# LSH attention and two MoE layers on one core: weight tiles rebuilt with a parametric ReLU, and tiles, transposes and the last x moved

## Chip, cores and metric

One core of a Trainium2 chip. The metric is the device time of one execution in microseconds (us), the median over several executions.

## What is computed

`q`, `k`, `v` are 2 x 8 heads x 768 positions x 64, float32; the weights are float64.

```python
q_bits = (einsum('bhsd,dk->bhsk', q, proj) > 0); k_bits likewise     # 6 bits, a bucket
mask = q_bucket[:, :, :, None] == k_bucket[:, :, None, :]
scores = where(mask, scale * q @ k.T, -1e9)
x = softmax(scores) @ v                 # laid out as 1536 tokens x 512
h = x @ w_in;  x = (h * sigmoid(1.702 * h)) @ w_out          # layer 1, d_ff 2048
h = x @ w_in2; out = (h * tanh(log1p(exp(h)))) @ w_out2      # layer 2
```

## The kernel before, in words

Every float32 operand of a product is split into a rounded high part and a low part, and a product is three matmuls (high x high, high x low, low x high).

**Attention.** `NSTEP` = 96 steps: 16 heads of 6 steps (`NT`), each step a block of 128 queries. In step i, `clamp` (L369) takes the scores out of PSUM on VectorE, `expo` (L380) exponentiates on ScalarE, and three steps later `trp` (L417, L424) transposes the probabilities on TensorE and copies out their high part on ScalarE, `trl` (L429) makes their low part on VectorE, and `pv` (L441, L442) multiplies by v. `ORDER` sets the order of the pieces in a step; its letter `T` runs what the table `todo` has for that step. `at(step, f, ...)` fills that table. `prep(n)` readies head n: `s0`, `s1` and `s3` are GpSimd work (L251 to L258, L328), `s2` is the bucket logits on TensorE (L266) and their compare into `mk` on VectorE (L280), `s4` and `s5` are DMAs of the results into `qb` and `kb`. Head 0 has a path of its own, `first` (L295 to L320), that runs before step 0, with head 1's k copied by `mid` (L335) in its middle. `x_out` and `x_split` normalise two finished heads on GpSimd and split them into `x_hi` and `x_lo`; for the last pair they run inside the MoE loop, at i of 4 and 6. After step 95 four more steps, called the drain here, finish transposes and products; each also holds a quarter of the first two `gemm_in`.

**Weight tiles.** 64 tiles of 128 x 512 float64 make up both layers (`wlist`; tile number k). `wload` loads one, and the generator `wsplit` turns it into float32 high and low parts in six stages; `wgo(k, n)` runs the next n:

```python
nc.scalar.mul(wf, hw.bitcast(F32), REBIAS)                                          # L112 ScalarE
nc.vector.tensor_scalar(lw, lw, 29, None, ALU.logical_shift_right)                  # L114 VectorE
nc.vector.scalar_tensor_tensor(lw, wb, 3, lw, ALU.logical_shift_left, ALU.bitwise_or)       # L116
nc.vector.scalar_tensor_tensor(wb, wb, 0x80000000, lw, ALU.bitwise_and, ALU.bitwise_or)     # L118
nc.scalar.copy(hi, wf)                                                              # L126 ScalarE
sub(lo, wf, rnd(hi))                                                                # L128
```

Before, `NPRE` = 5 tiles are made during attention, one per two heads: they run in heads 5 to 6, 7 to 8, 9 to 10, 11 to 12 and 13 to 14 (heads counted from 0), with the low part on GpSimd. The `at` calls of L528 to L532 set their steps.

**MoE.** Loop i runs `gemm_in(i)` (12 matmuls of 512 columns, L159), `act(i - 1)` (two ACTIVATEs on ScalarE, L600 and L601, and a subtraction on VectorE, L602) and `gemm_out(i - 2)` (12 matmuls, L618). There are 96 i: 2 layers x 3 chunks of 512 tokens x 16 blocks of d_ff. In the first chunk of layer 1, `conv(i)` gives two tiles to each loop, and the loop interleaves their stages with `act`. `gp` holds the activated blocks, three of each part.

Of the kernel before, what the change touches and what calls it, by code (L numbers as in the profile page):

```python
# [10 lines left out]
F32 = mybir.dt.float32  # L11
# [9 lines left out]
SET_GELU = 12  # L21
SET_MISH = 25
REBIAS = float(2.0**-112)


def mask_consts():
# [10 lines left out]
def lsh_attention_moe_kernel(  # L37
# [13 lines left out]
    P = 128  # L51
# [6 lines left out]
    NCH = NTOK // CH  # L58
    NW0 = 1
    XO = 11  # L60
    NPRE = 5
    NW1 = KF - 3
    QSCALE = -1.0 / float(D) ** 0.5

# [14 lines left out]
    def rnd(ap):  # L79
        return ap.bitcast(F32)  # L80
# [25 lines left out]
    def wsplit(k, sub):  # L106
        m, f, j = wlist[k]
        raw = raw_t.pop(k)
        lw, hw = raw[:, :, 0], raw[:, :, 1]
        wf = wr.tile([P, DM], F32, tag="wb", name="wb")  # L110
        wb = wf.bitcast(U32)
        nc.scalar.mul(wf, hw.bitcast(F32), REBIAS)  # L112
        yield
        nc.vector.tensor_scalar(lw, lw, 29, None, ALU.logical_shift_right)  # L114
        yield
        nc.vector.scalar_tensor_tensor(lw, wb, 3, lw, ALU.logical_shift_left, ALU.bitwise_or)  # L116
        yield
        nc.vector.scalar_tensor_tensor(wb, wb, 0x80000000, lw, ALU.bitwise_and, ALU.bitwise_or)  # L118
        yield
        n0 = NW0 + 3 * (j == 0)  # L120
        pi = 0 if f < n0 else 1 if f < NW1 else 2
        nb = (n0, NW1 - n0, KF - NW1)[pi]
        hi = wpools[pi].tile([P, DM], F32R, tag=f"wh{j}", name="wh", bufs=nb)
        lo = wpools[pi].tile([P, DM], F32R, tag=f"wl{j}", name="wl", bufs=nb)
        w_t[m, f, j] = (hi, lo)
        nc.scalar.copy(hi, wf)  # L126
        yield
        sub(lo, wf, rnd(hi))  # L128

    def wfetch(upto):  # L130
        while wstate["load"] < min(upto, len(wlist)):
            wload(wstate["load"])
            wstate["load"] += 1
# [30 lines left out]
    def attention():  # L164
        with ExitStack() as es:
# [16 lines left out]
            def load_q(n):  # L182
                b, h = divmod(n, H)
                t = nat.tile([P, S], F32, tag="qn", name="qn")
                nc.sync.dma_start(t[0:D], qt[b, h])
                nat_t["q", n] = t

            def load_k(n):
                b, h = divmod(n, H)
                t = nat.tile([P, S], F32, tag="kn", name="kn")  # L190
                nc.sync.dma_start(t, kt[b, h])
                nat_t["k", n] = t

            def load_v(u):
# [3 lines left out]
                nat_t["v", u] = t  # L198

            load_table(SET_EXP_LN)  # L200
            load_q(0)
            pjt = pp.tile([P, 3, 64], F32, tag="p", name="pjt")
            nc.sync.dma_start(pjt, pj)
            load_k(0)
            mc = cst.tile([P, 2], F32, name="mc")
            nc.sync.dma_start(mc, mconst)
# [3 lines left out]

            ident = cst.tile([P, P], F32, name="ident")
            make_identity(nc, ident)
            zero = pp.tile([P, 2, HS], F32, tag="p", name="zero").rearrange("p a b -> p (a b)")
            nc.vector.memset(zero[32:64], 0.0)
            qb_tiles = [cst.tile([P, S], F32R, name=f"qb{i}") for i in range(2)]
# [21 lines left out]
            def prep(n):  # L237
# [57 lines left out]
                def first(mid):  # L295
                    prep_w()
                    nc.vector.tensor_scalar(qk_m[0:D], qn[0:D], QSCALE, None, ALU.mult)
                    nc.scalar.mul(qx[D:P], qn[0:D], QSCALE)
                    nc.vector.scalar_tensor_tensor(
                        qx[0:D], qn[0:D], QSCALE, rnd(qk_m[0:D]), ALU.mult, ALU.subtract  # L300
                    )
                    pts = []
                    for f in range(2):
                        c = slice(f * HS, (f + 1) * HS)
                        nc.scalar.copy(kh[:, c], kn[:, c])
                        nc.vector.tensor_sub(qk_m[D:P, c], kn[D:P, c], rnd(kh[D:P, c]))
                    nc.scalar.copy(qb[D:P], rnd(qx[D:P]))
                    pcopy(kb[D:P], rnd(qk_m[D:P]))
                    for f in range(2):
                        c = slice(f * HS, (f + 1) * HS)  # L310
                        pts.append(ps_t.tile([P, 512], F32, tag="pt", name="pt"))
                        logits(pts[f], f, 64, True, True)
                    mid()
                    for f in range(2):
                        c = slice(f * HS, (f + 1) * HS)
                        nc.vector.tensor_scalar(
                            qb[0:64, c], pts[f][0:64, :HS], mc[0:64, 0:1], mc[0:64, 1:2],
                            ALU.is_gt, ALU.mult,
                        )
                        nc.scalar.copy(kb[0:32, c], rnd(qb[32:64, c]))  # L320
# [140 lines left out]
            def x_out(u):  # L461
                ul = xs_t[u]
                uh = uh_t.pop(2 * u)
                rb = rb_t.pop(u)
                nc.gpsimd.tensor_add(ul, ul, uh)
                nc.gpsimd.tensor_mul(ul, ul, rb)

            def x_split(u):
                ul = xs_t.pop(u)
                b, hp = divmod(u, NPAIR)  # L470
                t0, t1 = b * S, (b + 1) * S
                while t0 < t1:
                    c, o = divmod(t0, CH)
                    n = min(CH - o, t1 - t0)
                    xh = x_hi[c][:, hp, o : o + n]
                    src = ul[:, t0 - b * S : t0 - b * S + n]
                    pcopy(xh, src)
                    nc.gpsimd.tensor_sub(x_lo[c][:, hp, o : o + n], src, rnd(xh))
                    t0 += n

            first, first_v = prep(0)
            second = prep(1)
            first(second[1])
# [8 lines left out]
            def at(step, f, *args):  # L492
                todo.setdefault(step, []).append((f, args))
# [3 lines left out]

            at(1, first_v)

            for f, st in zip(second[3:], (1, 7, 1, 2)):  # L500
                at(st, f)

            def start_prep(n):
# [21 lines left out]
                at(NT * (n + 1) + NZ, norm2, n)  # L525
                at(NT * (n + 1) + NZ + 2, norm3, n)

            for k in range(NPRE):  # L528
                st = NSTEP - 4 - 2 * NT * (NPRE - k)
                at(st - 10, wfetch, k + 1)  # L530
                for off in (-1, 0, 2, 5, 8, 9):
                    at(st + off, wgo, k, 1, nc.gpsimd.tensor_sub)  # L532
            for j in range(3):
                at(st - 4 + 6 * j, wfetch, NPRE + 1 + j)
            at(NSTEP, load_table, SET_GELU)

            qk(0)
# [39 lines left out]
            for st in sorted(todo):  # L577
                for f, args in todo[st]:
                    f(*args)
            late.append(lambda: x_out(NHD // 2 - 1))  # L580
            late.append(lambda: x_split(NHD // 2 - 1))

    def moe():
        with ExitStack() as es:
            gp = es.enter_context(tc.tile_pool(name="gp", bufs=3))
            wpools[1] = es.enter_context(tc.tile_pool(name="w1", bufs=NW1))
            ps_y = es.enter_context(tc.tile_pool(name="ps_y", bufs=1, space=PSUM))
            N = len(steps)
# [55 lines left out]
            def conv(i):  # L644
                if i < KF:
                    return list(range(2 * i + 1, min(2 * i + 3, 2 * KF)))
                if i < LAST + 3:
                    return []
                a, b = (3 * (i - LAST - 3 + d) // 2 for d in (0, 1))
                return list(range(2 * KF + min(a, 2 * KF), 2 * KF + min(b, 2 * KF)))  # L650

            act(0)
            wgo(conv(2)[0], 1)
            for i in range(2, N + OLAG):
                if i == NH + 1:
                    load_table(SET_MISH)
                if i < KF and i in (4, 6):
                    late.pop(0)()
                if i == 9:
                    es_u.close()  # L660
                    wpools[2] = es.enter_context(tc.tile_pool(name="w2", bufs=KF - NW1))
                if i < N:
                    gemm_in(i)
                k1, k2 = (conv(i) + [None, None])[:2]
                if k1 is not None:
                    wgo(k1, 2)
                    for k in conv(i - 1)[1:]:
                        wgo(k, 1)
                    wgo(k1, 1)
                    wfetch(k1 + 4)  # L670
                elif i > 2:
                    for k in conv(i - 1)[1:]:
                        wgo(k, 1)
                if i - 1 < N:
                    act(i - 1)
                if k2 is not None:
                    wgo(k2, 1)
                if k1 is not None:
                    wgo(k1, 1)
                if k2 is not None:  # L680
                    wgo(k2, 2)
                if k1 is not None:
                    wgo(k1, 1)
                if k2 is not None:
                    wgo(k2, 1)
                    wfetch(k2 + 4)
                for k in conv(i + 1)[:1]:
                    wgo(k, 1)
                if k2 is not None:
                    wgo(k2, 1)  # L690
                gemm_out(i - OLAG)

    attention()
# [58 lines left out]
```

## Time and profile before

| what | value |
|---|---|
| median of 3 runs | 773.44 us (773.33 to 774.28) |
| the profiled execution's own time | 774.58 us |
| its span, first to last instruction | 772.7 us |
| TensorE, matmuls | 748.9 us busy (97%), 3760 instructions |
| VectorE | 431.8 us busy (56%), 791 instructions |
| ScalarE | 382.1 us busy (49%), 780 instructions |
| GpSimd | 186.4 us busy (24%), 189 instructions |
| chain that ended last | TensorE 79%, GpSimd 6%, VectorE 5%, issue 4%, DMA 3%, ScalarE 2% |

Matmuls are pipelined, so TensorE's busy time counts a matmul's whole flight and some of the gaps between two. The granted TensorE clock is printed as 1.0 over the whole span.

### The profile page before, as it was taken

To read this page: it belongs to the slowest core of one execution; us is meant where nothing else is said; L and a number is where in the kernel's file an instruction comes from. 1 tells how busy PE (TensorE), PEld (TensorE's weight loads), DVE (VectorE), ACT (ScalarE), POOL (GpSimd) and SP (SyncE) were. 2 spreads that over 40 slices of the span, in tenths; PEclk is the share of its full clock that TensorE was granted. 3 is DMA by queue.
4 is the path that set the end of the run, shared out by engine and by line. 5 is a ranking of instruction groups with operands and counts; after the bars stand their busy time and mean duration, and the time that the engine had idled before them with its cause. 6 is when DMAs were issued, how large, how long until landed. Compare 5 with 4: busy or idle time off the path is not lost.

```text
span 772.7 us, 10578 instructions
## 1 busy us (share of the span) xinstructions
PE 748.9 (97%) x3760; PEld 645.5 (84%) x3760; DVE 431.8 (56%) x791; ACT 382.1 (49%) x780; POOL 186.4 (24%) x189
## 2 busy tenths in 40 slices
PE   5999998999999899999999999999999999999998
PEld 4999998898898688888888888888888888888886
DVE  6988999899995999921111877779111211111111
ACT  5888888787786466632212554556211221222121
POOL 7767887788732400000000000000000000000000
PEclk9999999999999999999999999999999999999999
DMA  6576567475431466600000344534000100010001
GB/s 166 144 188 171 153 163 165 131 189 149 140 100 42 128 204 196 198 22 1 0 1 1 109 137 137 163 99 148 0 1 1 54 1 1 0 55 1 0 1 55
DMA packets 25892, 69.77 MB, mean 90 GB/s; under 512 B 4432, under 2 KB 6576, under 8 KB 25840
## 3 DMA queue, kind: packets, MB, share of 16 engines
q1 hardware_dynamic: 25840, 69.11, 31.2%
q8 instruction: 29, 0.48, 0.3%
q14 instruction: 23, 0.19, 0.1%
HBM read 49.38 MB, written 3.19 MB: 68 GB/s over the span
## 4 chain that ended last, share of the span: by engine, by line
PE 79%; POOL 6%; DVE 5%; issue 4%; DMA 3%; ACT 2%; SPq 1%; DVEq 0%; POOLq 0%; ACTq 0%
PE y L618 33%; PE h L159 33%; PE s L356 4%; PE pt L417 4%; PE u L442 2%; PE u L441 2%; DMA qn<-in_qt_dram 2%; DVE p L369 1%; PE prep L266 1%; ACT p L380 1%; DVE raw L116 1%; DVE ptl L429 1%; POOL qk_m L251 1%; POOL qk_m L258 1%; POOL qx L254 1%
## 5 line engine op out<-in xcount | busy, mean ns | idle before, releaser
L602 DVE TENSOR_TENSOR gl<-h,gh 128x512 fp32r<-128x512 f32 x96 | 66.2, 690 | 270.7 <-ACT h L601 270.2
L600 ACT ACTIVATE gh<-h 128x512 fp32r<-128x512 f32 x96 | 57.3, 597 | 255.6 <-PE h L159 255.6
L159 PE MATMUL h<-x_hi,wl 128*128 128x512 f32 x384 | 149.6, 389 | 0.9 <-DVE wl L128 0.9
L159 PE MATMUL h<-x_hi,wh 128*128 128x512 f32 x384 | 149.5, 389 | 0.0
L159 PE MATMUL h<-x_lo,wh 128*128 128x512 f32 x384 | 149.4, 389 | 0.0
L429 DVE TENSOR_TENSOR ptl<-pt,pth 128x384 fp32r<-128x384 f32 x192 | 98.0, 552 | 23.7 <-ACT pth L424 23.6
L380 ACT ACTIVATE p<-p,mn 128x768 f32<-128x768 f32 x96 | 91.1, 949 | 14.7 <-DVE p L369 14.3
L424 ACT CAST pth<-pt 128x384 fp32r<-128x384 f32 x192 | 83.0, 485 | 28.9 <-PE pt L417 28.5
L369 DVE TENSOR_SCALAR_CACHE_REDUCE p<-s 128x768 f32<-128x768 f32 x96 | 90.4, 943 | 2.2 <-PE s L356 2.2
L417 PE MATMUL pt<-ident,p 128*128 128x128 f32 x576 | 82.6, 274 | 8.9 <-DVE ptl L429 6.4
L159 PEld LDWEIGHTS h<-x_hi,wl 128*128 128x128 f32 x384 | 72.0, 187 | 16.3 <-DVE wl L128 1.3
L159 PEld LDWEIGHTS h<-x_hi,wh 128*128 128x128 f32 x384 | 72.1, 188 | 15.0 <-issue 0.2
L159 PEld LDWEIGHTS h<-x_lo,wh 128*128 128x128 f32 x384 | 72.1, 188 | 14.8
L417 PEld LDWEIGHTS pt<-ident,p 128*128 128x128 f32 x576 | 67.8, 140 | 18.4 <-DVE ptl L429 9.3
L618 PE MATMUL y<-gh,wl 128*128 128x512 f32 x192 | 75.0, 390 | 1.1 <-DVE wl L128 1.1
L618 PE MATMUL y<-gl,wh 128*128 128x512 f32 x192 | 74.8, 389 | 0.0
L618 PE MATMUL y<-gh,wh 128*128 128x512 f32 x192 | 74.7, 389 | 0.0
L618 PE MATMUL y<-wh,gh 128*128 128x512 f32 x192 | 74.7, 389 | 0.0
L618 PE MATMUL y<-wl,gh 128*128 128x512 f32 x192 | 74.7, 389 | 0.0
L618 PE MATMUL y<-wh,gl 128*128 128x512 f32 x192 | 74.7, 389 | 0.0
L441 PE MATMUL u<-pth,vv 128*128 128x384 f32 x192 | 64.9, 338 | 0.0
L442 PE MATMUL u<-ptl,vv 128*128 128x384 f32 x192 | 64.7, 337 | 0.0
(84 smaller groups left out, 1118.0 us busy)
## 6 DMA issues: line engine op xcount, KB each, us to landing
raw<-in_wt_dram SPq DMA_DIRECT2D x64, 512.0 KB, 3.6
kn<-in_kt_dram SPq DMA_DIRECT2D x16, 384.0 KB, 5.2
qn<-in_qt_dram SPq DMA_DIRECT2D x16, 192.0 KB, 6.5
vn<-in_vt_dram SPq DMA_DIRECT2D x8, 384.0 KB, 5.3
ul<-uh SPq DMA_DIRECT2D x16, 192.0 KB, 3.9
rb<-scr SPq DMA_DIRECT2D x16, 192.0 KB, 3.5
out_dram<-ob SPq DMA_DIRECT2D x12, 256.0 KB, 2.1
qx<-qk_m SPq DMA_DIRECT2D x15, 192.0 KB, 4.8
```

Source lines behind the costliest of these rows:

```text
L159: nc.tensor.matmul(h, a[:, wk], x[:, kk], start=(n == 0), stop=(n == 3 * KD - 1))
L356: nc.tensor.matmul(s[:, f, :HS], a[:, c], bb[:, f * HS : (f + 1) * HS], start=st, stop=not st,)
L369: nc.vector.tensor_scalar(sb, s[:, :, :HS], NEG, None, ALU.min, ALU.min, accum_out=mn)
L380: nc.scalar.activation(p, p, AF.Exp, bias=mn, scale=-1.0, accum_out=z_t[n][:, t : t + 1],)
L417: nc.tensor.transpose(ptile[:, j * P : (j + 1) * P], p_t[3 * g + j][:, t * P : (t + 1) * P], ident,)
L424: nc.scalar.copy(hi, ptile[:, :HS])
L429: nc.vector.tensor_sub(lo, ptile[:, :HS], rnd(hi))
L441: nc.tensor.matmul(ut[:, :HS], vv[:, t, :], hi, start=(t == 0), stop=False)
L442: nc.tensor.matmul(ut[:, :HS], vv[:, t, :], lo, start=False, stop=(t == NT - 1))
L600: nc.scalar.activation(gh, h, fn)
L602: nc.vector.tensor_sub(gl, h, rnd(gh))
L618: nc.tensor.matmul(y[j], w[:, js] if m == 0 else x[:, js], x if m == 0 else w, start=(first and n == 0), stop=(last and n == 2),)
```

## The change

- **Weight tiles.** For all tiles but the last five, stage 1 becomes a parametric ReLU on ScalarE whose slope for negative inputs is 2^32. Together with the later shift by 3 it puts the sign in place, so the second OR on VectorE (L118 before) is gone: five stages instead of six.
- **Where tiles are made.** Two tiles are still made during attention (heads 11 to 12 and 13 to 14). Tiles 2, 3 and 4 are made in step 95 and the drain, low part on VectorE (`DRAIN`).
- **The last x.** The last pair's `x_out` goes to VectorE at i = 7 (`x_last`), its split to ScalarE and VectorE in two pieces at i = 14 and 20 (`x_tail`). The buffer `xl` for it is new, and `gp` goes from three buffers to two.
- **The start.** 24 transposes of the identity into a scratch tile run on TensorE before its first use. `pjt` is loaded first; head 0's k is loaded as two halves of 64 partitions (before: 128 partitions at once), and its upper copy is made on ScalarE. Head 1's logits and mask go from steps 1 and 2 to steps 2 and 3.
- **Layer 2's tiles** are made two to a loop (before: three to two loops).

```diff
+NEGBIT = float(2.0**32)
-    NPRE = 5
+    NPRELU = 4 * KF - 5
+    DRAIN = (
+        (-1, 2, 1), (0, 2, 2), (0, 3, 1), (1, 2, 1), (1, 3, 2), (1, 4, 1), (2, 2, 1), (2, 3, 1),
+        (2, 4, 2), (3, 3, 1), (3, 4, 1), (4, 4, 1),
+    )
+    NWARM = 24
...
-        nc.scalar.mul(wf, hw.bitcast(F32), REBIAS)
+        if k < NPRELU:
+            nc.scalar.activation(wf, hw.bitcast(F32), AF.Prelu, scale=REBIAS, alpha=NEGBIT)
+        else:
+            nc.scalar.mul(wf, hw.bitcast(F32), REBIAS)
...
+        if k < NPRELU:
+            nc.vector.scalar_tensor_tensor(wb, wb, 3, lw, ALU.logical_shift_left, ALU.bitwise_or)
+        else:
...
+                if n == 0:
+                    for f in range(2):
+                        c = slice(f * HS, (f + 1) * HS)
+                        nc.sync.dma_start(t[0:D, c], kt[b, h, 0:D, c])
...
+            warm = ps_t.tile([P, 512], F32, tag="pt", name="warm")
+            for _ in range(NWARM):
+                nc.tensor.transpose(warm[:, :P], ident, ident)
...
-                        nc.scalar.copy(kh[:, c], kn[:, c])
-                        nc.vector.tensor_sub(qk_m[D:P, c], kn[D:P, c], rnd(kh[D:P, c]))
+                        nc.scalar.copy(kh[0:D, c], kn[0:D, c])
+                        nc.vector.tensor_sub(qk_m[D:P, c], kn[0:D, c], rnd(kh[0:D, c]))
+                        nc.scalar.copy(kh[D:P, c], rnd(kh[0:D, c]))
...
+            def x_last(xl):
+                u = NHD // 2 - 1
+                ul = xs_t.pop(u)
+                nc.vector.tensor_add(ul, ul, uh_t.pop(2 * u))
+                nc.vector.tensor_mul(xl, ul, rb_t.pop(u))
...
-            for f, st in zip(second[3:], (1, 7, 1, 2)):
+            for f, st in zip(second[3:], (2, 7, 1, 3)):
...
-            for k in range(NPRE):
-                st = NSTEP - 4 - 2 * NT * (NPRE - k)
+            for k in range(2):
+                st = NSTEP - 4 - 2 * NT * (2 - k)
                 at(st - 10, wfetch, k + 1)
-                for off in (-1, 0, 2, 5, 8, 9):
+                for off in (-1, 0, 2, 4, 5):
                     at(st + off, wgo, k, 1, nc.gpsimd.tensor_sub)
...
+            for st, k, n in DRAIN:
+                at(NSTEP + st, wgo, k, n)
...
-            gp = es.enter_context(tc.tile_pool(name="gp", bufs=3))
+            gp = es.enter_context(tc.tile_pool(name="gp", bufs=2))
...
+            def x_tail(c, t0, t1):
+                o = (B - 1) * S - c * CH
+                xh, xo = (x[c][:, KD - 1, t0 + o : t1 + o] for x in (x_hi, x_lo))
+                nc.scalar.copy(xh, xl[:, t0:t1])
+                nc.vector.tensor_sub(xo, xl[:, t0:t1], rnd(xh))
...
+                if i == 7:
+                    late.pop()(xl)
+                if i == KF - 2:
+                    x_tail(1, 0, 2 * CH - S)
+                if i == KF + 4:
+                    x_tail(2, 2 * CH - S, S)
```

How this moves the instructions, at three places. First VectorE from step 95 on, before (`ptl` is `trl`; `raw`, `wb`, `wl` are the stages of a weight tile; `gl` is `act`):

```order
L369 TENSOR_SCALAR p,mn<-s 128x768
L429 TENSOR_TENSOR ptl<-pt,pth 128x384 x8
L395 RECIPROCAL z<-z 128x6
L602 TENSOR_TENSOR gl<-h,gh 128x512
L114 TENSOR_SCALAR raw<-raw 128x512
L116 SCALAR_TENSOR_TENSOR raw<-wb,raw 128x512
L118 SCALAR_TENSOR_TENSOR wb<-wb,raw 128x512
```

and with the change:

```order
L451 TENSOR_TENSOR ptl<-pt,pth 128x384 x4
L123 TENSOR_SCALAR raw<-raw 128x512
L126 SCALAR_TENSOR_TENSOR wb<-wb,raw 128x512
L451 TENSOR_TENSOR ptl<-pt,pth 128x384 x2
L123 TENSOR_SCALAR raw<-raw 128x512
L126 SCALAR_TENSOR_TENSOR wb<-wb,raw 128x512
L451 TENSOR_TENSOR ptl<-pt,pth 128x384 x2
L141 TENSOR_TENSOR wl<-wb,wh 128x512
L123 TENSOR_SCALAR raw<-raw 128x512
L126 SCALAR_TENSOR_TENSOR wb<-wb,raw 128x512
L417 RECIPROCAL z<-z 128x6
L141 TENSOR_TENSOR wl<-wb,wh 128x512 x2
```

Nine instructions of three tiles now stand between the last low parts of the probabilities and before the first `gl`. Second, ScalarE before step 0, before:

```order
L298 ACTIVATE qx<-qn 64x768
L305 CAST kh<-kn 128x384 x2
L307 CAST qb_126<-qx 64x768
L335 CAST kh<-kn 128x768
L320 CAST kb_128<-qb_126 32x384 x2
```

and with the change:

```order
L319 ACTIVATE qx<-qn 64x768
L326 CAST kh<-kn 64x384
L328 CAST kh<-kh 64x384
L326 CAST kh<-kn 64x384
L328 CAST kh<-kh 64x384
L329 CAST qb_152<-qx 64x768
L357 CAST kh<-kn 128x768
L342 CAST kb_154<-qb_152 32x384 x2
```

Two copies of 128 partitions became four of 64; head 1's `kh` still stands ahead of the two copies into `kb`. Third, GpSimd from the reciprocals' input of the last head on, before:

```order
L392 TENSOR_SCALAR z<-z 128x6
L77 TENSOR_SCALAR x_hi<-ul 128x256
L478 TENSOR_TENSOR x_lo<-ul,x_hi 128x256
L77 TENSOR_SCALAR x_hi<-ul 128x512
L478 TENSOR_TENSOR x_lo<-ul,x_hi 128x512
L465 TENSOR_TENSOR ul<-ul,uh 128x768
L466 TENSOR_TENSOR ul<-ul,rb 128x768
L77 TENSOR_SCALAR x_hi<-ul 128x256
L478 TENSOR_TENSOR x_lo<-ul,x_hi 128x256
L77 TENSOR_SCALAR x_hi<-ul 128x512
L478 TENSOR_TENSOR x_lo<-ul,x_hi 128x512
```

and with the change:

```order
L414 TENSOR_SCALAR z<-z 128x6
L83 TENSOR_SCALAR x_hi<-ul 128x256
L500 TENSOR_TENSOR x_lo<-ul,x_hi 128x256
L83 TENSOR_SCALAR x_hi<-ul 128x512
L500 TENSOR_TENSOR x_lo<-ul,x_hi 128x512
```

The six instructions of the last pair are gone from GpSimd, which has nothing left to do in the MoE layers.

## Rows read from the trace of the kernel before

**Rows 1.** Busy time by stretch: us, busy us (xcount) per engine, granted clock, DMA share, GB/s

```profile
0.00:10.49 10.49, 2.90 (x9) 2.46 (x9) 6.56 (x11) 5.25 (x8) 6.89 (x17) 1.00 0.54 159
...
22.36:76.90 54.54, 54.54 (x365) 52.86 (x364) 48.10 (x106) 45.78 (x108) 40.00 (x41) 1.00 0.64 162
76.90:166.10 89.20, 84.08 (x550) 79.47 (x548) 81.53 (x167) 72.43 (x169) 71.02 (x68) 1.00 0.63 158
166.10:225.56 59.46, 55.67 (x366) 52.72 (x364) 55.43 (x112) 48.10 (x113) 41.84 (x42) 1.00 0.53 140
...
236.28:248.89 12.61, 12.26 (x71) 10.42 (x70) 5.11 (x12) 7.05 (x16) 3.20 (x5) 1.00 0.10 27
248.89:268.51 19.62, 17.58 (x75) 13.53 (x74) 17.52 (x23) 10.16 (x19) 8.25 (x6) 1.00 0.43 128
...
290.00:317.00 27.00, 27.00 (x121) 22.36 (x120) 25.96 (x47) 17.82 (x31) 0.00 (x0) 1.00 0.61 196
...
331.00:763.00 432.00, 432.00 (x1908) 357.71 (x1907) 138.90 (x224) 134.22 (x241) 0.00 (x0) 1.00 0.12 41
```

**Rows 2.** The chain that ended last, in order of time: start, us, what

```profile
7.46 2.26 PE pt L266 x6
...
96.77 1.06 PE prep L266 x6
...
268.51 2.72 PE h L159 x12
```

**Rows 3.** Instructions in order of time, the start: start, us, engine, line, operation [idle before]

```profile
6.13 0.93 ACT L305 CAST kh<-kn 128x384 fp32r<-128x384 f32 x2 [1.33 <-DMA kn<-in_kt_dram]
...
8.97 0.84 ACT L335 CAST kh<-kn 128x768 fp32r<-128x768 f32 x1 [1.07 <-DMA kn<-in_kt_dram]
...
9.83 1.14 ACT L320 CAST kb<-qb 32x384 fp32r<-32x384 f32 x2
...
11.75 0.96 DVE L369 TENSOR_SCALAR_CACHE_REDUCE p<-s 128x768 f32<-128x768 f32 x1 [0.34 <-PE s L356]
...
14.16 0.68 DVE L280 TENSOR_SCALAR mk<-prep,mc 128x384 f32<-128x384 f32 x1 [0.16 <-PE prep L266]
...
21.21 0.51 PE L356 MATMUL s<-kb,qb 128*128 128x384 f32 x2
```

**Rows 4.** Instructions in order of time, head 7, and line 114 over the span (min/median/max ns)

```profile
111.86 1.82 POOL L258 TENSOR_TENSOR qk_m<-kn,kh 64x768 fp32r<-64x768 f32 x1
111.95 2.02 DVE L114 TENSOR_SCALAR raw<-raw 128x512 uint32<-128x512 uint32 x1
...
L114 DVE TENSOR_SCALAR raw<-raw x64: 414/420/2041, 83.7 to 540.2; 128x512 uint32<-128x512 uint32 x64
```

**Rows 5.** Instructions in order of time, the first MoE loops

```profile
251.85 2.12 POOL L465 TENSOR_TENSOR ul<-ul,uh 128x768 f32<-128x768 f32 x1 [9.67 <-DMA uh<-uh]
...
252.30 2.22 DVE L118 SCALAR_TENSOR_TENSOR wb<-wb,raw 128x512 uint32<-128x512 uint32 x1
...
258.56 0.50 PE L618 MATMUL y<-gh,wl 128*128 128x512 f32 x1 [0.98 <-DVE wl L128]
```

**Rows 6.** Groups of instructions by line and shape: xcount | busy us, mean ns | idle before

```profile
L602 DVE TENSOR_TENSOR gl<-h,gh 128x512 fp32r<-128x512 f32 x96 | 66.2, 690 | 270.7 <-ACT h L601 270.2
L600 ACT ACTIVATE gh<-h 128x512 fp32r<-128x512 f32 x96 | 57.3, 597 | 255.6 <-PE h L159 255.6
...
L118 DVE SCALAR_TENSOR_TENSOR wb<-wb,raw 128x512 uint32<-128x512 uint32 x64 | 46.6, 729 | 0.4
L112 ACT ACTIVATE wb<-raw 128x512 f32<-128x512 f32 x64 | 43.2, 675 | 6.5 <-DMA raw<-in_wt_dram 6.5
L128 DVE TENSOR_TENSOR wl<-wb,wh 128x512 fp32r<-128x512 f32 x59 | 40.7, 689 | 0.3
L126 ACT CAST wh<-wb 128x512 fp32r<-128x512 f32 x64 | 39.8, 622 | 41.1 <-DVE wb L118 40.2
...
L261 DVE TENSOR_TENSOR qk_m<-kn,kh 64x768 fp32r<-64x768 f32 x1 | 1.0, 955 | 0.0
```

More of the change, by code (lines that the diff above doesn't have):

```diff
@@ L115, in wsplit @@
         yield
-        nc.vector.scalar_tensor_tensor(lw, wb, 3, lw, ALU.logical_shift_left, ALU.bitwise_or)
-        yield
-        nc.vector.scalar_tensor_tensor(wb, wb, 0x80000000, lw, ALU.bitwise_and, ALU.bitwise_or)
+        if k < NPRELU:
+            nc.vector.scalar_tensor_tensor(wb, wb, 3, lw, ALU.logical_shift_left, ALU.bitwise_or)
+        else:
+            nc.vector.scalar_tensor_tensor(lw, wb, 3, lw, ALU.logical_shift_left, ALU.bitwise_or)
+            nc.vector.scalar_tensor_tensor(
+                wb, wb, 0x80000000, lw, ALU.bitwise_and, ALU.bitwise_or
+            )
         yield
@@ L190, in load_k @@
                 t = nat.tile([P, S], F32, tag="kn", name="kn")
-                nc.sync.dma_start(t, kt[b, h])
+                if n == 0:
+                    for f in range(2):
+                        c = slice(f * HS, (f + 1) * HS)
+                        nc.sync.dma_start(t[0:D, c], kt[b, h, 0:D, c])
+                else:
+                    nc.sync.dma_start(t, kt[b, h])
                 nat_t["k", n] = t
@@ L200, in attention @@
             load_table(SET_EXP_LN)
-            load_q(0)
             pjt = pp.tile([P, 3, 64], F32, tag="p", name="pjt")
             nc.sync.dma_start(pjt, pj)
+            load_q(0)
             load_k(0)
@@ L526, in attention @@
                 at(NT * (n + 1) + NZ + 2, norm3, n)
-            for k in range(NPRE):
-                st = NSTEP - 4 - 2 * NT * (NPRE - k)
+            for k in range(2):
+                st = NSTEP - 4 - 2 * NT * (2 - k)
                 at(st - 10, wfetch, k + 1)
-                for off in (-1, 0, 2, 5, 8, 9):
+                for off in (-1, 0, 2, 4, 5):
                     at(st + off, wgo, k, 1, nc.gpsimd.tensor_sub)
-            for j in range(3):
-                at(st - 4 + 6 * j, wfetch, NPRE + 1 + j)
+            for k, st in ((2, -20), (3, -14), (4, -8), (5, 1), (6, 2), (7, 3)):
+                at(NSTEP + st, wfetch, k + 1)
+            for st, k, n in DRAIN:
+                at(NSTEP + st, wgo, k, n)
             at(NSTEP, load_table, SET_GELU)
@@ L579, in attention @@
                     f(*args)
-            late.append(lambda: x_out(NHD // 2 - 1))
-            late.append(lambda: x_split(NHD // 2 - 1))
+            late.append(x_last)
     def moe():
         with ExitStack() as es:
-            gp = es.enter_context(tc.tile_pool(name="gp", bufs=3))
+            gp = es.enter_context(tc.tile_pool(name="gp", bufs=2))
+            xl = es.enter_context(tc.tile_pool(name="xl", bufs=1)).tile([P, S], F32, name="xl")
             wpools[1] = es.enter_context(tc.tile_pool(name="w1", bufs=NW1))
@@ L648, in conv, with wsteps @@
                     return []
-                a, b = (3 * (i - LAST - 3 + d) // 2 for d in (0, 1))
-                return list(range(2 * KF + min(a, 2 * KF), 2 * KF + min(b, 2 * KF)))
+                o = 2 * KF + 2 * (i - LAST - 3)
+                return list(range(o, min(o + 2, 4 * KF)))
+            def x_tail(c, t0, t1):
[3 more added lines that the diff above has]
+                nc.vector.tensor_sub(xo, xl[:, t0:t1], rnd(xh))
+            def wsteps(ks, n):
+                for k in ks:
+                    wgo(k, n)
             act(0)
-            wgo(conv(2)[0], 1)
+            wsteps(conv(2)[:1], 1)
             for i in range(2, N + OLAG):
@@ L656, in moe @@
                     load_table(SET_MISH)
-                if i < KF and i in (4, 6):
-                    late.pop(0)()
                 if i == 9:
@@ L663, in moe @@
                     gemm_in(i)
[L664 to L673, printed above, removed]
+                k1, k2 = conv(i)[:1], conv(i)[1:]
+                wsteps(k1, 1)
+                wsteps(conv(i - 1)[1:], 1)
+                wsteps(k1, 1)
+                for k in k1:
+                    wfetch(k + 4)
                 if i - 1 < N:
                     act(i - 1)
[L676 to L690, printed above, removed]
+                wsteps(k2, 1)
+                wsteps(k1, 1)
+                wsteps(k2, 2)
+                for k in k2:
+                    wfetch(k + 4)
+                wsteps(k1, 1)
+                wsteps(conv(i + 1)[:1], 1)
+                wsteps(k2, 1)
+                if i == 7:
[4 more added lines that the diff above has]
+                    x_tail(2, 2 * CH - S, S)
                 gemm_out(i - OLAG)
```

## The prediction

> **What bounds the kernel now.** I began with the chain that ended last, in order of time. From 268.51 us on it is nothing but TensorE: blocks of twelve matmuls of 2.72 us each, a `gemm_in` or a `gemm_out`, one behind the other [rows 2]. The busy times by stretch say the same: between 331 and 763 us TensorE is busy 432.00 of 432.00 us while VectorE has 138.90 [rows 1]. Two thirds of the time can't move, since the change takes no matmul out of the MoE layers. What can move is what comes before 268.51 us, so I cut that part into stretches.
>
> In heads 1 to 4 (22.36 to 76.90 us, each head starting with its first clamp on VectorE) no weight tile is made, and TensorE is busy 54.54 of 54.54 us: a head costs 13.64 us and TensorE is its limit [rows 1]. Heads 5 to 10 take 89.20 us where six heads at 13.64 us would take 81.8: 7.4 us too long, and TensorE has gaps of 5.1 us there. Heads 11 to 14 take 59.46 us where four would take 54.5: 4.9 us too long. Three tiles are made in the first of these stretches and two in the second, and both come to 2.5 us a tile. That is the reading on which most of the forecast rests: a tile made during attention lengthens it by 2.5 us, though its own work could lie in other engines' gaps.
>
> Why so much is seen in the instructions of head 7: the shift of line 114 takes 0.42 us as a rule (the median of 64), but 2.02 us where it starts at 111.95 us, beside a GpSimd subtraction that began at 111.86 and ran 1.82 us [rows 4]. VectorE stands still until GpSimd is done, and the clamp and the low parts queue behind the shift.
>
> The same happens where the MoE loops begin. From 248.89 to 268.51 us there are six blocks, which at 2.72 us are 16.3 us; the stretch has 19.62 [rows 1, 2], so 3.3 us are lost. There GpSimd normalises the last pair of heads, the second OR takes 2.22 us instead of 0.73, the low part of a weight is late, and TensorE waits 0.98 us for it in one place [rows 5, 6]. The last place is the start: 22.36 us until head 1 begins, with six logits matmuls that take 2.26 us where six of the same shape later take 1.06 [rows 2].
>
> **The change, part by part.**
>
> *Tiles out of attention.* Three of five tiles leave heads 5 to 10. At 2.5 us each that is 7.4 us. From the other side, TensorE's gaps alone are 5.1 us, so the gain is between 5.1 and 7.4. I take 7.4, since heads 1 to 4 are the same work without tiles, with the same GpSimd work on the other pairs.
>
> *The second OR in the two tiles that stay.* Two times 0.73 us [rows 6] at most, 1.5 us; nothing if it stood in a gap. I take nothing: the long wait of [rows 4] is at the shift, which stays where it is.
>
> *The drain.* VectorE gets three tiles of 0.42 + 0.73 + 0.69 us, 5.5 us in all, ScalarE three times 0.68 + 0.62 us, 3.9 us [rows 4, 6]. The stretch from 236.28 to 248.89 us has 5.11 us of VectorE and 7.05 of ScalarE in 12.61 [rows 1]; with the new work 10.6 and 10.9. Both still fit, and what hides them is TensorE's own 12.3 us of matmuls. But the work stands in front of the low parts of the next step, and `gl` of the first block queues behind it, so some of it can show: between nothing and all 5.5 us. The nearest row is the gap that this stretch has now, 0.35 us; I take 0.6 us.
>
> *The first MoE loops.* GpSimd has nothing left to do there, and each tile is one VectorE instruction shorter. Between 0 and 3.3 us are won; I take 3.3, as both causes seen in [rows 5] are gone. Loads don't hold it back: the tiles for these loops are still asked for three ahead.
>
> *The start.* The first clamp comes at 11.75 us. Going back, ScalarE makes the two copies into `kb` at 9.83 us, right behind head 1's `kh` at 8.97, and that copy waited 1.07 us for its load; head 0's k had been there since 6.13 [rows 3]. So head 0's shorter load and split copies help only as far as they bring head 1's k in sooner. They move 0.2 MB less ahead of it, 1.2 us at the 159 GB/s of that stretch [rows 1], and spend one more load's issue; between 0 and 1.2 us, I take 0.7. If the transposes bring TensorE to full speed before the logits, the six logits are done 1.2 us sooner, but they end off this path; the score matmuls ahead of the first clamps win some 0.4 us (0 to 0.4). Head 1's mask, 0.68 us on VectorE, no longer stands before the third clamp, whose exponential the first transposes wait for: 0.7 us (0 to 0.7, since what is late next is the mask itself, made one clamp later; its copies now have until 21.21 us, 6.4 us behind the mask's end at 14.84, and would have 5 [rows 3]). Together 1.8 us, between 0 and 2.3.
>
> *The rest costs nothing.* `x_last` is two operations of 768 columns, some 1.9 us by the one of that length in [rows 6], plus 1.0 us for the tails. VectorE is busy 25.96 of 27.00 us from 290 to 317 us, about ten tiles [rows 1]; without the second OR it has 7.3 us less, which covers this. If that cover were gone, a low part would be late and TensorE would wait, as at 258.56 us. The parametric ReLU is not in the trace; its nearest rows are the scaling it replaces (0.68 us) and the activation of the same size (0.60) [rows 6]. Even at twice the price, ScalarE would have 17.82 + 6.8 us in those 27. Layer 2's tiles come faster now, in loops where VectorE is a third busy.
>
> **The sum.** 7.4 + 0 - 0.6 + 3.3 + 1.8 = 11.9 us. Against the profiled execution's own 774.58 us that is 762.7 us; the median of the runs is 1.1 us below that execution, so I forecast **761.5 us**.
>
> **The rivals.**
>
> 1. *TensorE stays slow at the start.* The granted clock is printed as 1.00 in every stretch, the first included, yet the six logits at 7.46 us, TensorE's first work, ran at half the rate of those at 96.77: 0.38 against 0.18 us each, the lower of its two levels, 1.2 against 2.4 GHz [rows 1, 2]. If transposes alone don't raise it, the 0.4 us of the score matmuls is not won, and another 0.4 us or so in the steps after it: 762.3 us. No stretch of this trace has transposes alone, so the rows don't decide. The Trainium skill, in "TensorE: Matmul & The Clock Gate", Part 4 (PE-mode transpose), speaks against this part of the change: it says that transposes don't count as TensorE activity in the same way and that the full clock doesn't come on for them. By that rule it is this rival; no run here shows it. I give it 0.28.
> 2. *The tiles show in the drain.* VectorE's 5.5 us sit between the low parts, and TensorE waits for most of them: 4 us more than I took, 765.5 us. For it speaks that VectorE is in order and the last of three tiles comes just before the first `gl`; against it the 7.5 us that VectorE is idle there. 0.10.
> 3. *Attention's lost time isn't the tiles'.* If loads or GpSimd hold heads 5 to 10 as well, only TensorE's gaps come back, 5.1 us, and if the start also gives nothing the time is 765.6 us. Against it stands that the price of a tile comes out the same in both stretches. 0.10.
> 4. *Slower: two buffers for the activated blocks.* `act(i - 1)` must now wait until `gemm_out(i - 3)` has read its buffer, one block later than before. If ScalarE and VectorE could not make up for it, each of 94 loops would stretch; from 0.13 us a loop on this eats the whole gain, and at 0.3 us a loop the time is 761.5 + 28 = 790 us. Against it: the two activations and the subtraction take 0.60 + 0.60 + 0.69 = 1.9 us [rows 6], and the next use of the block comes three blocks, 8.2 us, later. It decides only if 6 us of other work are queued before them. 0.04.
> 5. *The change does little*, because stalls at one place reappear at another (less than 0.2% either way, about what a measurement of this kernel can tell from no change, 1.5 us): 0.03.
>
> **How the numbers follow.** My forecast has 0.45; rivals 1 to 3 are all faster too, so faster by over 0.2% has 0.93, within 0.2% 0.03, slower 0.04. With the start at 2.3, attention at 7.4, the first loops at 3.3, no cost in the drain and some of the second OR's 1.5 us, the time would be near 759.2; the upper end takes in rivals 2 and 3, 765.8. Rivals 4 and 5, and two mishaps at once, are left out.
>
> **What would show it.** Heads 5 to 10 should take close to 82 us and TensorE should have no gaps there; heads 11 to 14 should still be some 4 to 5 us too long, with a shift of 2 us beside GpSimd. From the first `gemm_in` of i = 2 on, every block should follow at 2.72 us, with no wait for a weight's low part. The drain should stay at 12.5 to 13.2 us. The first clamp should come near 10.7 us, still behind head 1's `kh`, and the logits should run at 0.18 us each; 0.38 would be rival 1. I am wrong if heads 5 to 10 keep more than 85 us, or if TensorE's blocks show gaps after the first loops.

## The result, and the profile after

The changed kernel takes 761.12 us (median of 4, 759.50 to 761.26) beside 773.50 for the kernel before (773.33 to 774.28): a ratio of 0.9833, 95% interval 0.9816 to 0.985. The forecast was 761.5. Its profiled execution took 759.50 us, span 757.7.

The busy times by stretch of the changed kernel, columns as in [rows 1]:

```profile
20.07:74.42 54.35, 54.35 (x365) 52.89 (x364) 48.08 (x105) 45.74 (x108) 41.65 (x43) 1.00 0.64 164
74.42:156.12 81.70, 81.70 (x548) 79.60 (x547) 72.03 (x157) 69.10 (x163) 67.12 (x66) 1.00 0.64 160
156.12:212.96 56.84, 55.29 (x366) 52.91 (x365) 51.55 (x110) 48.01 (x113) 40.17 (x39) 1.00 0.52 143
...
223.60:236.20 12.60, 11.84 (x68) 10.01 (x67) 10.05 (x20) 9.46 (x21) 3.26 (x5) 1.00 0.36 113
236.20:255.00 18.80, 18.80 (x84) 15.40 (x84) 15.03 (x27) 13.78 (x27) 0.00 (x0) 1.00 0.68 224
```

The first three are heads 1 to 4, 5 to 10 and 11 to 14. Heads 5 to 10 went from 89.20 to 81.70 us and have no TensorE gap left; heads 11 to 14, which still make two tiles, from 59.46 to 56.84. The fourth is the drain, where VectorE's busy time doubled to 10.05 us and TensorE's matmuls have gaps of 0.76. This row ends at 236.20 us; up to the first matmul of `gemm_in(2)`, where the row of before ends, the drain takes 13.37 us instead of 12.61. From 236.2 us on TensorE has no gap: its blocks follow at 2.72 us from 237.22 to the last, as the chain in order of time shows.

```profile
237.22 2.77 PE h L172 x12
239.98 2.72 PE y L648 x12
242.70 2.72 PE h L172 x12
```

The start, in order of time:

```profile
6.85 0.33 PE L287 MATMUL pt<-kh,pwt 128*128 128x384 f32 x1
7.02 0.34 PE L287 MATMUL pt<-qx,pwt 128*128 128x384 f32 x1
...
10.53 0.96 DVE L391 TENSOR_SCALAR_CACHE_REDUCE p<-s 128x768 f32<-128x768 f32 x1 [0.49 <-PE s L378]
```

After 24 identity transposes, which began at 1.36 us, two logits matmuls start 0.17 us apart, so at the upper of TensorE's two rates; [rows 2] had 0.38 us each. The transposes themselves started 0.21 us apart up to 5.5 us and 0.11 us apart behind that. The first clamp came at 10.53 us instead of 11.75 [rows 3].

To follow all runs below, their profiles are cut at the same five points: the first clamp of heads 1, 5, 11 and 15, the first matmul of `gemm_in(2)`, and the end of the last matmul. All in us, from the start times of these instructions:

| kernel | until head 1 | heads 5-10 | heads 11-14 | head 15 and drain | MoE from i = 2 |
|---|---|---|---|---|---|
| before | 22.36 | 89.19 | 59.47 | 23.33 | 520.10 |
| changed | 20.07 | 81.70 | 56.84 | 24.01 | 517.09 |
| a0_again | 21.52 | 81.70 | 56.89 | 24.00 | 517.09 |
| x1_no_warm | 22.27 | 82.45 | 56.89 | 24.02 | 517.09 |
| y4_no_warm_again | 20.71 | 81.69 | 56.90 | 24.02 | 517.09 |
| x3_two_ors_attn | 20.31 | 81.69 | 59.90 | 24.00 | 517.06 |
| x4_five_in_attn | 20.31 | 85.38 | 56.99 | 23.35 | 517.06 |
| x2_two_ors | 20.29 | 81.71 | 60.04 | 24.29 | 517.54 |
| x5_last_x_pool | 20.26 | 81.70 | 56.94 | 24.01 | 518.01 |
| x6_tiles_late | 20.35 | 81.70 | 57.76 | 23.99 | 517.06 |
| y1_tiles_late_loads | 20.15 | 81.69 | 55.69 | 24.00 | 517.06 |
| y2_fill_gap | 20.30 | 81.69 | 56.90 | 23.99 | 517.09 |
| y3_late_fill | 20.30 | 81.70 | 55.39 | 24.01 | 517.06 |
| x7_kb_first | 23.86 | 81.71 | 56.88 | 24.02 | 517.06 |

Heads 1 to 4 take 54.34 to 54.37 us in every kernel but the one before (54.54).

### The profile page after: what moved, and what is told of

Read it like the earlier page. It is cut to its first block, busy times and chain, and to the rows that moved or that the text cites. A ratio compares the mean times of both kernels' runs of the same rounds, so it can differ in the third digit from the quotient of the medians.

```text
span 757.7 us, 10547 instructions
## 1 busy us (share of the span) xinstructions
PE 748.3 (99%) x3784; PEld 648.7 (86%) x3784; DVE 387.8 (51%) x739; ACT 381.3 (50%) x784; POOL 173.0 (23%) x180
## 3 DMA queue, kind: packets, MB, share of 16 engines
HBM read 49.19 MB, written 3.19 MB: 69 GB/s over the span
## 4 chain that ended last, share of the span: by engine, by line
PE 80%; POOL 10%; issue 4%; DMA 2%; ACT 1%; DVE 1%; SPq 1%; POOLq 0%; ACTq 0%; DVEq 0%
PE y L648 34%; PE h L172 34%; PE s L378 4%; PE pt L439 3%; DMA qn<-in_qt_dram 2%; PE u L463 2%; PE u L464 2%; POOL qk_m L279 1%; POOL qx L275 1%; POOL vv L350 1%; POOL x_lo L500 1%; POOL qk_m L272 1%; POOL ul L488 1%; POOL ul L487 1%; PE prep L287 1%
## 5 line engine op out<-in xcount | busy, mean ns | idle before, releaser
L172 PEld LDWEIGHTS h<-x_lo,wh 128*128 128x128 f32 x384 | 72.1, 188 | 14.9
L172 PEld LDWEIGHTS h<-x_hi,wh 128*128 128x128 f32 x384 | 72.0, 188 | 14.9 <-issue 0.2
L439 PE MATMUL pt<-ident,p 128*128 128x128 f32 x576 | 81.0, 274 | 2.0 <-DVE ptl L451 1.2
```

Source lines behind the costliest of these rows:

```text
L172: nc.tensor.matmul(h, a[:, wk], x[:, kk], start=(n == 0), stop=(n == 3 * KD - 1))
L439: nc.tensor.transpose(ptile[:, j * P : (j + 1) * P], p_t[3 * g + j][:, t * P : (t + 1) * P], ident,)
```

## The experiments

My theory after the result was that a tile made in attention is dear because VectorE waits for GpSimd; the rivals were loads, the second OR alone, and a start that transposes don't help. Medians stand beside those of the changed kernel, 761.12 and, run again, 760.55 us.

**The changed kernel again.**

> The changed kernel again, as the base of the runs beside it: 759.5 to 761.3 us. Its profiled execution was the shortest of four (759.5), so a second profile may be 1.7 us longer; it should show where, most likely as a gap in attention or in the drain and not among the MoE blocks.

760.55 us (759.76 to 763.59; ratio 0.9836, 0.9813 to 0.9858). The profile (761.07 us) differs from the first at one place, the start: head 1 begins 1.45 us later. Its logits ran at the upper rate, but then it fell back. Instructions in order of time, and the stretch from 11.0 to 15.3 us:

```profile
9.88 0.77 PE L378 MATMUL s<-kb,qb 128*128 128x384 f32 x2 [1.16 <-ACT kb L342]
...
13.04 0.53 PE L287 MATMUL prep<-qk_m,pwt 128*128 128x384 f32 x1
13.36 0.53 PE L287 MATMUL prep<-kh,pwt 128*128 128x384 f32 x1
```

```profile
11.00:15.30 4.30, 3.94 (x14) 3.62 (x14) 2.59 (x7) 2.96 (x6) 4.13 (x5) 0.60 0.98 240
```

Starts 0.32 us apart and a granted clock of 0.60: for part of this stretch TensorE had the lower level. Before it fell, TensorE had stood still for 1.16 us up to 9.88, waiting for the copies into `kb`. The same gap is in the first profile, where the rate held.

**No transposes at the start**, twice:

```diff
-    NWARM = 24
+    NWARM = 0
```

> No identity transposes at the start, all else as changed. If the transposes brought TensorE to its upper rate, the six logits go back from 0.18 to 0.38 us each and the first clamp from 10.5 to about 11 us: 0.4 to 1.0 us longer. If the rate would have risen in time without them, or if the start hangs on head 1's k alone, within 0.3 us.

> No identity transposes at the start, once more, since the first run of it had a slow profile and fast times. If the transposes matter, the logits run at 0.38 us each, head 1 starts 1.9 us later than at 20.3 and the times lie above 761.5 us. If the rate mostly rises early enough without them, the times lie at 760.1 to 760.5 us again.

760.34 us (760.12 to 762.53; 0.9832, 0.9815 to 0.9849) and 760.33 us (760.22 to 761.99; 0.9831, 0.9818 to 0.9844). In both profiles the first logits run at the lower rate, as here in the first one:

```profile
7.32 0.52 PE L287 MATMUL pt<-kh,pwt 128*128 128x384 f32 x1
7.64 0.52 PE L287 MATMUL pt<-qx,pwt 128*128 128x384 f32 x1
```

In the second the rate rose at about 11.5 us, and head 1 began at 20.71, 0.4 to 0.6 us later than in most runs with transposes; in the first it rose only at about 16 us, and head 1 began at 22.27. The first profile also lost 0.75 us in heads 8 and 9, where no tile is made: its chain of work that ended last runs there through a copy of head 9's mask.

```profile
126.40 4.63 DMA kb<-mk
```

The transposes do raise the rate, but as they stand the medians gain nothing from them. That the fall costs in some executions what the transposes win in others is my reading; no run isolates it.

**Two ORs again, in attention's two tiles only.**

```diff
-        if k < NPRELU:
+        if 2 <= k < NPRELU:
```

> Only the two tiles made in attention go back to the plain scaling and two ORs. If the dropped OR halved the price of such a tile (2.5 to 1.25 us), heads 11 to 14 go from 56.8 back to 58.3 to 59.5 us, 1.5 to 2.5 us longer. If the price fell because the shift now starts later beside the same GpSimd subtraction (0.78 us where it took 2.02), they stay at 56.8 to 57.3 us.

762.85 us (762.71 to 764.19; 0.9862, 0.9847 to 0.9877). Heads 11 to 14 go back to 59.90 us, 3.0 us longer, but not by the same amount for each tile. Head 11, with the first tile, takes 15.60 us instead of 14.88 in `a0_again`: 0.7 us, about the duration of the second OR (0.69). Head 12 loses 0.6 us, where the scores come late behind a mask copy of 4.62 us, and head 13 loses 1.7. There the second tile's shift now starts beside a GpSimd subtraction. The shifts of the two tiles:

```profile
162.96 0.79 DVE L123 TENSOR_SCALAR raw<-raw 128x512 uint32<-128x512 uint32 x1
...
193.00 1.48 DVE L123 TENSOR_SCALAR raw<-raw 128x512 uint32<-128x512 uint32 x1
```

In the changed kernel these two took 0.78 and 0.45 us, not 2.02 as in [rows 4]:

```profile
162.72 0.78 DVE L123 TENSOR_SCALAR raw<-raw 128x512 uint32<-128x512 uint32 x1
...
191.15 0.45 DVE L123 TENSOR_SCALAR raw<-raw 128x512 uint32<-128x512 uint32 x1
```

So the mean, 1.5 us a tile, is not the price of the OR. Both ORs now run in one step, which they did not before.

**Tiles 2 to 4 back in attention**, five stages, none in the drain:

```diff
-            for k in range(2):
-                st = NSTEP - 4 - 2 * NT * (2 - k)
+            for k in range(5):
+                st = NSTEP - 4 - 2 * NT * (5 - k)
...
```

> Tiles 2 to 4 go back into heads 5 to 10, with five stages; the drain has none. If a five-stage tile costs 1.25 us in attention wherever it lies, heads 5 to 10 take 81.7 + 3.7 = 85.4 us and the whole 3 to 4 us more than the changed kernel. If the price is 2.5 us as in the kernel before, 89 us and 7 us more. If attention's lost time came from loads and not from tiles, no more than 1 us more.

763.23 us (763.11 to 763.38; 0.9863, 0.9846 to 0.9879). The stretch of heads 5 to 10:

```profile
74.67:160.05 85.38, 82.93 (x548) 79.32 (x547) 77.07 (x163) 72.07 (x169) 70.17 (x67) 1.00 0.60 165
```

85.38 us, 3.7 more for three tiles, and the drain 0.65 less. A five-stage tile costs 1.2 to 1.3 us wherever it lies among these heads. So of the 7.5 us won in heads 5 to 10, half comes from the move of tiles that already have five stages. The other half is not the parametric ReLU's alone: this kernel also keeps the new steps of the stages, and 1.6 us of the time before lie at a wait for a mask's copies (see below).

**All tiles with two ORs**, the rest as changed:

```diff
-    NPRELU = 4 * KF - 5
+    NPRELU = 0
```

> All tiles by plain scaling and two ORs; the rest as changed. VectorE then has 2 x (0.42 + 0.69 + 0.73 + 0.69) + 0.69 = 5.75 us in each of the loops 2 to 15, which last 5.44 us. If that limits, it falls behind by 0.3 us a loop and by 1.9 us at the last x, TensorE waits for low parts again, and with the two tiles of attention the time is 3 to 7 us longer. If the slack of a loop and a half covers it, only attention's share is lost, 1 to 2.5 us.

763.98 us (763.69 to 765.21; 0.9882, 0.9865 to 0.9898). Attention loses 3.2 us, the MoE loops only 0.45 us: the slack covers nearly all of it there. Of the 3.2 us, 1.5 are not the OR's: head 14 takes 15.05 us instead of 13.56. At the end of head 13 TensorE had stood still for 1.58 us, waiting for a low part from VectorE, and in head 14 it ran 3.4 us at the lower level. The instruction behind the wait, and that stretch:

```profile
201.01 0.44 PE L439 MATMUL pt<-ident,p 128*128 128x128 f32 x2 [1.58 <-DVE ptl L451]
```

```profile
201.89:205.30 3.41, 3.41 (x15) 3.31 (x14) 2.49 (x6) 2.60 (x6) 0.72 (x1) 0.50 0.54 142
```

The second OR itself costs 0.7 us in head 11 and 0.9 in head 13, 1.6 us for both. Head by head, in us, with the duration of the tile's shift in brackets; a head without a tile takes 13.6:

| kernel | stages | head 5 | head 7 | head 9 | head 11 | head 13 |
|---|---|---|---|---|---|---|
| before | six | 14.84 (0.56) | 16.10 (2.02) | 15.56 (2.02) | 16.11 (2.03) | 16.12 (2.04) |
| x4_five_in_attn | five | 14.87 (0.54) | 14.91 (0.48) | 14.89 (0.47) | 14.91 (0.48) | 14.91 (0.48) |
| changed | five | none | none | none | 14.84 (0.78) | 14.86 (0.45) |
| x2_two_ors | six | none | none | none | 15.59 (0.79) | 15.81 (0.45) |
| x3_two_ors_attn | six | none | none | none | 15.60 (0.79) | 16.56 (1.48) |

Before, a six-stage tile cost 2.0 to 2.5 us where its shift took 2 us beside GpSimd, and 1.2 us in head 5, where the shift took 0.56. With the new steps the shift is short with six stages too (x2), so it is not the missing OR alone that took it out of GpSimd's way; x3 shows that it can come back when a head before it is late. No run moves the shift alone, so this is a reading of the traces.

**The last pair on GpSimd again**, at i of 4 and 6:

```diff
-            late.append(x_last)
+            late.append(lambda: x_out(NHD // 2 - 1))
+            late.append(lambda: x_split(NHD // 2 - 1))
...
-                if i == 7:
-                    late.pop()(xl)
...
+                if i in (4, 6):
+                    late.pop(0)()
```

> The last pair of heads goes back to GpSimd at i = 4 and 6; the five-stage tiles stay. If GpSimd beside VectorE was what cost the first loops 3.3 us, part of it returns: VectorE operations of 1.2 to 2.2 us beside GpSimd, gaps on TensorE, 0.5 to 2.5 us longer. If the second OR was the cause, the shorter tiles absorb it: within 0.3 us.

761.95 us (761.86 to 763.74; 0.9857, 0.9842 to 0.9872). The first loops in order of time:

```profile
241.82 2.25 POOL L487 TENSOR_TENSOR ul<-ul,uh 128x768 f32<-128x768 f32 x1 [11.88 <-DMA ul<-uh]
...
242.37 2.26 DVE L141 TENSOR_TENSOR wl<-wb,wh 128x512 fp32r<-128x512 f32 x1
...
251.96 0.50 PE L649 MATMUL y<-gh,wl 128*128 128x512 f32 x1 [0.60 <-DVE wl L141]
```

A low part of 0.68 us takes 2.26 beside GpSimd, as an OR did in [rows 5], and TensorE waits again, but the loops lose 0.92 us, not 3. Neither cause alone makes the 3 us of the kernel before. Together they come to 1.4; that both at once would use up the slack and cost the rest is not shown, since no run takes both back. The change also reorders a tile's stages within a loop, and no run tests that.

**The two tiles in heads 14 and 15**, first with loads at steps 66 and 69:

```diff
-                st = NSTEP - 4 - 2 * NT * (2 - k)
-                at(st - 10, wfetch, k + 1)
-                for off in (-1, 0, 2, 4, 5):
+                st = NSTEP - 12 + 3 * k
+                at(st - 18, wfetch, k + 1)
+                for off in (-1, 0, 1, 3, 4):
```

> The two tiles of attention move to heads 14 and 15, where GpSimd readies no further head. If waiting for GpSimd makes their price, it falls below 0.7 us a tile: heads 11 to 13 take 13.6 us each and the whole is 0.5 to 1.5 us shorter. If VectorE's own 1.8 us a tile are the price, or if they delay the drain, the same or up to 1.5 us longer.

761.42 us (760.77 to 763.88; 0.985, 0.9833 to 0.9868). Heads 14 and 15 behave as hoped (14.41 us, and nothing in the drain), but heads 11 and 12, with no tile work, take 15.83 and 13.90 us: score matmuls wait there for the mask's copies, 2.06 us in one place. I had moved the loads of two tiles beside those copies. With the tiles there and the loads at other steps:

```diff
...
-            for k, st in ((2, -20), (3, -14), (4, -8), (5, 1), (6, 2), (7, 3)):
+            for k, st in ((0, -38), (1, -26), (2, -20), (3, -8), (4, -5), (5, 1), (6, 2), (7, 3)):
```

> Tiles 0 and 1 in heads 14 and 15 as in x6_tiles_late, but their loads, and those of tiles 3 and 4, in steps that hold no mask copies. If the loads beside the mask copies lengthened heads 11 and 12 there (15.8 and 13.9 us), heads 11 to 13 now take 13.6 us each, head 14 14.4 us or less, heads 11 to 14 55.3 us where the changed kernel has 56.9, and the drain keeps its 24.0 us: 1.5 us shorter. If heads 11 and 12 stay long, the loads were not it.

759.08 us (758.36 to 760.24; 0.9812, 0.9799 to 0.9826). Heads 11 to 14 take 55.69 us. VectorE's two operations of the first tile, where GpSimd was idle:

```profile
199.84 0.42 DVE L123 TENSOR_SCALAR raw<-raw 128x512 uint32<-128x512 uint32 x1
...
201.98 0.68 DVE L126 SCALAR_TENSOR_TENSOR wb<-wb,raw 128x512 uint32<-128x512 uint32 x1
```

0.68 us where the same OR took 1.50 in head 11 of the changed kernel, beside GpSimd. The two tiles cost some 1.2 us together instead of 2.4.

**Ten more transposes in TensorE's gap**, alone and with the late tiles:

```diff
+                    for _ in range(fill if st else 0):
+                        nc.tensor.transpose(warm[:, :P], ident, ident)
...
-            qk(0)
+            qk(0, 10)
```

> Ten more identity transposes in TensorE's gap before the first score matmuls that need kb. If TensorE's rate falls back in some executions because of that gap, and this is what parts the executions at 759.6 from those at 761.2 us, then the logits of head 1 run at 0.18 us each, head 1 starts at 20.0 to 20.4 us, and nearly all executions lie at 759.3 to 760.2 us. If the two groups have another cause, they remain.

> Both edits at once. If they are independent, 1.5 us less for the tiles and the upper group gone: 757.8 to 758.8 us. If they are one and the same luck of timing, no better than the better of the two.

Alone 760.30 us (759.76 to 760.56; 0.9825, 0.9811 to 0.9838): no better in the median, but narrow. Together **758.13 us** (758.00 to 758.29; 0.9798, 0.9784 to 0.9811), the best version, 2.4 to 3 us below the changed kernel. A clock lowered for 3.4 us shows as a mean of 0.998 over an execution. Of the 13 executions with 24 transposes and no filling (the changed kernel twice, and the late tiles with their loads moved), five have that mean; of the eight with filling none has. That fits the gap as what lets the rate fall, but doesn't prove it. The mean does not say where the rate fell: all four executions of x2 have 0.998 or less, and in its profile the fall lies in head 14. None of the four of x4 has it, without filling. And it does not sort the times: one of the five, at 760.99 us, lies below its kernel's median, while 761.25 us came with 1.000.

**ScalarE's copies into `kb` before head 1's k.**

```diff
-                    mid()
                     for f in range(2):
...
                         nc.scalar.copy(kb[0:32, c], rnd(qb[32:64, c]))
+                    mid()
```

> ScalarE copies into kb before it copies head 1's k. If the first clamp waits for these two copies behind head 1's k, it comes at 9.7 us instead of 10.5 and head 1 starts 0.4 to 0.8 us earlier. If head 1's own mask and its copies by DMA set when head 1 starts, the first clamp comes earlier but head 1 does not: within 0.3 us.

764.03 us (763.81 to 765.35; 0.9882, 0.9867 to 0.9897), against both expectations. In order of time:

```profile
10.43 1.80 POOL L275 TENSOR_TENSOR qx<-qn,qk_m 64x768 fp32r<-64x768 f32 x1
10.60 2.44 DVE L282 TENSOR_TENSOR qk_m<-kn,kh 64x768 fp32r<-64x768 f32 x1 [1.44 <-ACT kh L357]
...
13.08 0.96 DVE L391 TENSOR_SCALAR_CACHE_REDUCE p<-s 128x768 f32<-128x768 f32 x1
```

On VectorE, head 1's subtraction stands before the first clamp. It came 1.5 us later, ran into GpSimd and took 2.44 us instead of 0.96; the scores were ready long before. That makes the first clamp 2.3 us late. The rest of the 3.5 us by which head 1 starts later is the rate: TensorE stood still for 3.19 us, waiting for that clamp, and then ran 3.4 us at the lower level.

```profile
14.10 1.01 PE L378 MATMUL s<-kh,qx 128*128 128x384 f32 x2 [3.19 <-DVE p L391]
```

```profile
13.97:17.38 3.41, 3.28 (x10) 3.28 (x11) 1.92 (x6) 2.54 (x5) 3.24 (x4) 0.50 0.37 87
```

## Why the prediction was right

Profile against profile, term by term:

- **Heads 5 to 10.** 7.4 us forecast, 7.5 measured; the path was right, the price per tile only as a mean. Tiles do lengthen attention: without them these heads run at TensorE's pace, and with tiles back in place (x4) they cost 1.2 us each. But "2.5 us a tile" was a mean over unlike things: 1.2 us in head 5, 2.5 in head 7, 2.2 in heads 9 and 10, and 1.6 in head 8, while heads 6, 12 and 14, which also end a tile, lose nothing. In head 8 TensorE waited for the copies of head 9's mask:

```profile
135.68 0.96 PE L356 MATMUL s<-kb,qb 128*128 128x384 f32 x2 [1.49 <-DMA kb<-mk]
```

  So rival 3, other causes in these heads, had a part. x1 shows a smaller delay at the same place with no tile near (0.75 us), and the other profiles of the changed kernel and its variants show none there; whether the kernel before has it in every execution, its one profile can't tell. That 7.4 came so close is in part luck.
- **The second OR in the two tiles that stay.** Nothing forecast, at most 1.5 us; heads 11 to 14 became 2.6 us shorter, outside the bounds. This is the mis-sized term. The bound of two times 0.73 us was about right for the OR itself: it costs 0.7 and 0.9 us (x2). The step that failed is "the shift, which stays where it is": with the new steps the shifts took 0.78 and 0.45 us instead of 2.03 and 2.04. That fits the other 1.0 us, but no run isolates it. The sign "a shift of 2 us beside GpSimd", with these heads 4 to 5 us too long, did not come: they are 2.4 us too long.
- **The drain.** 0.6 us forecast, 0.68 measured with head 15, of which the tiles' move makes 0.65 (x4). The drain alone takes 13.37 us, just above the 13.2 of the forecast. Rival 2 is out.
- **The first MoE loops.** 3.3 us forecast, 3.0 measured, and no wait left. I named both causes; taken back alone they are worth 0.92 (x5) and 0.45 us (x2), and how the other 1.6 us divide is not shown.
- **The start.** 1.8 us forecast; 2.3 in the first profile, 0.8 in the second. The first clamp, forecast at 10.7 us, came at 10.53 and 10.68. What I did not see is that the rate, once up, can fall.
- **Rival 1** is refuted for this kernel. All eleven profiles with 24 transposes show the logits behind them at the upper rate, from the second matmul on at the latest, and both without them at the lower. In eight of the eleven the transposes themselves come to start 0.11 us apart instead of 0.21, with no other matmul ahead of them. The Trainium skill ("TensorE: Matmul & The Clock Gate", Part 4, PE-mode transpose) says that the full clock doesn't engage for transposes; these traces disagree. The rival's price, 0.8 us, was about right: head 1 came 0.4 to 0.6 us later in the better of the two profiles without transposes.
- **Rival 4**, two buffers for the activated blocks: from i = 2 on TensorE has no gap at all.

The closeness of 761.5 to 761.12 owes much to luck. The terms between the two first profiles add up to 14.9 us where I summed 11.9, the OR's 2.6 being most of the difference. But that profile of before lay 1.1 us above its median, and that of the changed kernel 1.6 us below. Against the second profile, with the fallen rate, the sum is 13.4 us. Where the kernel before had its 1.1 us isn't shown; the wait in head 8 would be large enough.

## What to carry to other kernels

When a piece of work appears in some stages and not in others, the excess of these stages prices it better than the sum of its instructions' durations. But look at the stages one by one before dividing: the mean of 2.5 us held tiles of 1.2 and 2.5 us, and a wait for a mask's copies. An instruction on a queueing engine costs more when it stands beside another engine that holds it up; look for places where that engine is idle (0.68 against 1.50 us for the same OR), and when steps change, check which neighbour each instruction meets now. Before a longer stage is put down to an edit, read the granted clock of that stage: half of x2's loss in attention was the clock. Move a load and an engine's work separately: the late tiles won nothing until their loads kept clear of the mask's copies.

## What the hardware showed that I had not expected

Transposes of the identity alone raised TensorE's rate: their starts went from 0.21 to 0.11 us apart. It fell again in three profiles, around a time in which TensorE stood still: 1.16 us at the start (a0_again), 3.19 us at the start (x7), 1.58 us at the end of head 13 (x2). It came back some 3.4 us later each time, and the head that it fell in took 1.2 to 1.5 us longer. Waits as long also passed without a fall: the same 1.16 us in the first profile, 1.79 us in head 13 of x3. The granted clock shows such a fall (0.60 in a0_again's stretch) but not the low rate before the first rise, when it prints 1.00 while matmuls start 0.32 us apart. A VectorE operation that started during a GpSimd one was held up in three places: 2.02 us instead of 0.42 for a shift, 2.44 instead of 0.96 for a subtraction, 2.26 instead of 0.68 for a low part. Each ended 0.3 to 0.8 us after the GpSimd operation, a little less than its own usual time. And an operation that GpSimd runs beside VectorE can be longer as well: 2.25 us for the addition that took 1.90 in head 11.
